# P times V in three fused layers: from two fp32r products with split operands to one float32 product, two heads on the two 64-column halves of TensorE

## The chip, the cores and the metric

One core of a Trainium2 chip runs the whole program. The metric is device time in microseconds (us), taken as the median of several runs. The engines are named as in the profile: PE is TensorE (its matmuls), PEld its weight loads, DVE is VectorE, ACT is ScalarE, POOL is GpSimd, and SP is SyncE, which here only issues DMAs.

## What is computed

Three layers follow one another: an attention whose keys are masked by a hash, a mixture of four causal attention experts (moe), and a mixing layer with sines (moe2). In short form:

```python
def _attn_ref(q, k, v, proj):            # q, k, v: (2, 8, 768, 64), proj: (64, 6)
    q_bits = (np.einsum('bhsd,dk->bhsk', q, proj) > 0)
    k_bits = (np.einsum('bhsd,dk->bhsk', k, proj) > 0)
    mask = q_bucket[:, :, :, None] == k_bucket[:, :, None, :]
    scores = np.where(mask, scale * np.matmul(q, k.transpose(0, 1, 3, 2)), -1e9)
    attn = np.exp(scores - scores.max(-1)); attn /= attn.sum(-1) + 1e-09
    return np.matmul(attn, v)
def _moe_ref(x, w_gate, wq, wk, wv, wo): # x: (2, 768, 512), four experts of width 64
    for e in range(4):                   # causal attention of each expert, two of four kept
        ye = softmax(causal(q @ k.T)) @ v @ wo[e]
        out += gate(x, e) * ye
def _moe2_ref(x, w_theta, w_tok_r, w_tok_i, w_ch):
    theta = x @ w_theta
    y = w_tok_r @ (x * cos(theta)) + w_tok_i @ (x * sin(theta))
    return (x + y) + np.maximum((x + y) @ w_ch, 0.0)
```

## The kernel before

**Two heads are a group.** The attention has 2 batches of 8 heads, so 8 groups; the moe has 2 batches of 4 experts, so 4 groups. A group has 6 row blocks of 128 queries for each head (or expert), called side 0 and side 1. A `Unit` is one such row block in the attention; in the moe it is one row block of each side, whose widths differ because of the causal mask.

**What a unit does.** `scores` (L2009) multiplies queries and keys in PSUM with operands in fp32r, each number split into a high and a low part that are packed into the 128 rows of one operand; 12 further rows hold the hash bits of q and k, so that the mask comes out of the same product. `low` (L2018, DVE) scales the scores and takes the row's extreme, `exp` (L2027, ACT) makes P. `flip` (L2035) transposes P block by block on PE into PSUM. `split_hi` (L2046, ACT) rounds the transposed P to fp32r as PTh, `split_lo` (L2049, DVE) writes the rest as PTl. `mix` (L2065, PE) multiplies: V is stationary with 128 columns, 64 of its high part and 64 of its low part, and PTh and PTl stream through it in turn, 256 columns (two row blocks) at a time. So the result O holds, for one head, two halves of 64 partitions that still have to be added. `gather` copies O out of PSUM (ACT), `swap` (L1959, a DMA on SP's queue) brings one half onto the other's partitions, and `add` (L1963, mostly POOL) adds them into `bt`. `scale`, `spread` and `finish` divide by the sums.

**Preparation.** For each pair of heads `Prep` loads q, k and v, splits q and k on POOL, computes the hash with 8 fp32r matmuls (L2220: high and low parts of q and k against split projection weights), turns it into bits on ACT (L2222), DVE (L2224) and POOL (L2225), splits V into its high and low halves on POOL (`values`, L2233 and L2234), and packs the operands with DMAs on SP's queue (L2243). The very first pair is handled apart (`first_head`); its hash is the one place where PE multiplies plain float32 (L2161 to L2186). In the moe, `values_b` splits V on ACT and DVE, and for batch 0 both are parked in DRAM (`v_d`).

**What sets the order.** The program text gives a default order of jobs (`fill`, `ORD`). A planner (`Plan`) then reads all instructions with prices for each kind (`price`), schedules them by list with a rank of how far each lies from the end, and fixes the order on every engine. A long table `NUDGES` shifts the ranks of instructions in certain stretches of time before the last pass of that planner. Pools of tiles limit what may be alive: three PSUM tiles `ps`, two tiles `O`, two pairs PTh and PTl. Idle places of PE at the very start are filled with 38 spare matmuls (L1902).

## Time and profile before

| | |
|---|---|
| time, median of 3 runs | 530.48 us (530.31 to 530.82) |
| span of the profiled execution | 527.9 us, so some 2.6 us of the median lie around it |
| PE busy (ends modelled) | 520.5 us, 99% |
| PEld (weight loads, beside PE) | 458.9 us, 87% |
| DVE / ACT / POOL busy | 427.0 / 370.7 / 294.6 us |
| L2065, P times V on PE | 768 matmuls |
| L2049 and L2046, the split of P transposed | 116.6 us of DVE, 97.9 us of ACT |
| L1963, the adding of the halves | 42.4 us of POOL |

Matmuls are pipelined: one of 256 columns has a record of about 0.3 us, but the next begins some 0.12 us later. So PE's busy share says little, and the distance from start to start says what a matmul costs. The view that shows it is the chain of work that ended last, where matmuls in a row are merged with their number. The stages are: attention up to about 260 us (with the projections of the first moe batch inside it), the moe up to about 355 us, then the mixing layer.

### The profile page before, as it was taken

Reading aid. Unit: us, or ns where it says so; the run is one execution under the profiler, and the core shown is the slowest. Engines: PE = TensorE matmul, PEld = TensorE weight load, DVE = VectorE, ACT = ScalarE, POOL = GpSimd, SP = SyncE. Lnnn points to the kernel's source line nnn. Section 1 sums busy time; section 2 is a strip of 40 time slices with the busy share of each in tenths; the row PEclk is TensorE's granted clock in tenths of the full one; section 3 lists DMA queues with packets and bytes.
Section 4 is the critical chain, followed back from the end, with each engine's and each line's share of the span. In section 5 each row is a group of like instructions: output and inputs, shape, how many; then the busy total and the mean of one; then the engine's idle time right before and its main releaser. Section 6 shows DMA issues by size and latency. Waiting matters only on the chain.

```text
span 527.9 us, 9485 instructions
## 1 busy us (share of the span) xinstructions
PE 520.5 (99%) x3341; PEld 458.9 (87%) x3341; DVE 427.0 (81%) x707; ACT 370.7 (70%) x691; POOL 294.6 (56%) x248
## 2 busy tenths in 40 slices
PE   9999999999999999999999999999999999999997
PEld 5999999979999999999898998878888778888886
DVE  6898988898987699888967988988989999924343
ACT  7888888888755588778968668996775667553110
POOL 6988998539504798824230204746766487955000
PEclk9999999999999999999999999999999999999999
DMA  6774644637477764795716533653445343350012
GB/s 205 194 191 143 170 131 108 181 73 194 135 257 241 236 190 128 181 243 135 196 54 188 144 122 97 178 156 91 112 117 170 120 120 120 88 153 20 20 61 99
DMA packets 33287, 76.04 MB, mean 144 GB/s; under 512 B 6000, under 2 KB 7664, under 8 KB 33240
## 3 DMA queue, kind: packets, MB, share of 16 engines
q1 hardware_dynamic: 31080, 71.94, 48.8%
q10 hardware_dynamic: 2160, 3.50, 1.8%
q8 instruction: 26, 0.43, 0.3%
q14 instruction: 21, 0.17, 0.1%
HBM read 44.67 MB, written 14.32 MB: 112 GB/s over the span
## 4 chain that ended last, share of the span: by engine, by line
PE 89%; DVE 3%; ACT 2%; issue 2%; DMA 2%; POOL 1%; POOLq 0%; ACTq 0%
PE ps L2638 18%; PE ps L2009 15%; PE O L2065 15%; PE ps L2035 14%; PE ps L2357 6%; PE wk L2552 5%; PE wk L2567 4%; PE ps L2292 3%; PE ps L2567 3%; PE ps L2220 2%; PE ps L2499 1%; DMA raw<-in_wtok_dram 1%; PE spare L1902 1%; DMA bt<-ob 1%; PE wk L2651 1%
## 5 line engine op out<-in xcount | busy, mean ns | idle before, releaser
L2018 DVE TENSOR_SCALAR_CACHE_REDUCE ss<-ps 128x768 f32<-128x768 f32 (+3 forms) x144 | 119.3, 840 | 26.2 <-PE ps L2009 16.2
L2027 ACT ACTIVATE ss<-ss,m 128x768 f32<-128x768 f32 (+4 forms) x144 | 122.3, 850 | 15.3 <-DVE ss L2018 14.7
L2049 DVE TENSOR_TENSOR PTl<-ps,PTh 128x768 fp32r<-128x768 f32 x120 | 116.6, 980 | 10.9 <-ACT PTh L2046 10.5
L2046 ACT CAST PTh<-ps 128x768 fp32r<-128x768 f32 x120 | 97.9, 819 | 29.6 <-PE ps L2035 23.5
L2035 PE MATMUL ps<-ident,ss 128*128 128x128 f32 x744 | 109.7, 273 | 0.8 <-DVE PTl L2049 0.6
L2065 PE MATMUL O<-PTh,V 128*128 128x256 f32 (+1 forms) x384 | 104.7, 296 | 0.0
L2065 PE MATMUL O<-PTl,V 128*128 128x256 f32 (+1 forms) x384 | 103.4, 293 | 0.0
L1963 POOL TENSOR_TENSOR bt<-bt,ob 64x768 f32<-64x768 f32 x23 | 42.4, 1845 | 86.8 <-DMA bt<-ob 37.3
L2035 PEld LDWEIGHTS ps<-ident,ss 128*128 128x128 f32 x744 | 85.8, 140 | 4.3 <-PE O L2065 0.6
L2638 PE MATMUL ps<-zh,tok 128*128 128x512 f32 x240 | 77.8, 394 | 0.0
L2065 PEld LDWEIGHTS O<-PTh,V 128*128 128x128 f32 x384 | 72.6, 189 | 2.1 <-ACT PTh L2046 0.2
L2065 PEld LDWEIGHTS O<-PTl,V 128*128 128x128 f32 x384 | 72.9, 190 | 1.5
L2009 PE MATMUL ps<-op 76*128 76x256 f32 (+5 forms) x256 | 63.8, 341 | 0.2 <-DVE PTl L2049 0.2
L2638 PEld LDWEIGHTS ps<-zh,tok 128*128 128x128 f32 x240 | 44.8, 188 | 9.3
L2638 PE MATMUL ps<-zl,tok 128*128 128x512 f32 x120 | 46.7, 396 | 0.5 <-DVE zl L2599 0.5
L1834 POOL TENSOR_TENSOR tok<-raw,tok 128x512 fp32r<-128x512 f32 x27 | 40.7, 1518 | 8.6 <-ACT tok L1831 6.5
L2009 PEld LDWEIGHTS ps<-op 128*128 128x128 f32 (+1 forms) x256 | 41.0, 190 | 3.5 <-DVE PTl L2049 0.4
L2638 PEld LDWEIGHTS ps<-zl,tok 128*128 128x128 f32 x120 | 22.5, 188 | 6.0 <-DVE zl L2599 1.3
L2027 ACT ACTIVATION_READ_ACCUMULATOR ss<-ss,m 128x1 f32 x144 | 27.5, 191 | 0.0
L1808 DVE SCALAR_TENSOR_TENSOR g<-raw,g 128x512 uint32<-128x512 uint32 x26 | 26.8, 1032 | 0.4
L2587 POOL TENSOR_TENSOR kk<-kk,x 128x512 f32<-128x512 f32 x12 | 17.3, 1443 | 17.4 <-ACT kk L2586 14.0
L1809 DVE SCALAR_TENSOR_TENSOR g<-raw,g 128x512 uint32<-128x512 uint32 x26 | 25.5, 981 | 0.5
(241 smaller groups left out, 1100.9 us busy)
## 6 DMA issues: line engine op xcount, KB each, us to landing
raw<-in_wtok_dram SPq DMA_DIRECT2D x18, 512.0 KB
raw<-tok_d SPq DMA_DIRECT2D x27, 256.0 KB
bt<-ob SPq DMA_DIRECT2D x24, 192.0 KB
tok_d<-g SPq DMA_DIRECT2D x18, 256.0 KB
op<-qk_d SPq DMA_DIRECT2D x24, 192.0 KB
rT<-r_d SPq DMA_DIRECT2D x20, 192.0 KB
raw<-in_vP_dram SPq DMA_DIRECT2D x8, 384.0 KB
qk_d<-op SPq DMA_DIRECT2D x8, 384.0 KB
```

Of the source, the lines that this page charges most:

```text
L1834: nc.gpsimd.tensor_sub(l, raw, f(h))
L1963: engine.tensor_add(self.bt[keep], self.bt[keep], self.ob[keep, side])
L2009: nc.tensor.matmul(self.sp[:, c0:c1], lhs, rhs[:, c0 - off:c1 - off], start=a == 0, stop=last)
L2018: i = nc.vector.tensor_scalar(self.ss[:, off:off + w], self.sp[:, off:off + w], -0.125, NEG, op0=OP.mult, op1=OP.min, accum_out=m)
L2027: e = nc.scalar.activation(self.P[:, off:off + w], self.ss[:, off:off + w], AF.Exp, bias=m, scale=-1.0, accum_out=self.grp.den[:, side, i: ...
L2035: nc.tensor.transpose(self.pt[:, j * 128:(j + 1) * 128], self.P[:, j * 128:(j + 1) * 128], ident)
L2046: nc.scalar.copy(self.d[0], self.v)
L2049: nc.vector.tensor_sub(self.d[1], self.v, f(self.d[0]))
L2065: nc.tensor.matmul(o, g.V[:, j, side, :], rhs, start=j == 0 and a == 0, stop=j == w // 128 - 1 and a == 1)
L2357: nc.tensor.matmul(pp[:, c0:c1], lhs[:, kd, e, :], rhs[kd][:, c0:c1], start=n == 0, stop=n == 3 * NK - 1)
L2567: nc.tensor.matmul(o, lhs[:, sl], rhs[:, kd, cols], start=n == 0, stop=n == 3 * NK - 1)
L2638: nc.tensor.matmul(yp[t], lhs[:, a, t, :], rhs[:, a], start=i == 0 and a == 0 and n == 0, stop=i == NT - 1 and a == 1 and n == 2)
```

## The change

**P times V.** Transposed P is copied once, as float32, from PSUM to a tile PT (`copy`): of three units two are copied by ACT and one by DVE. V is not split: the attention loads it straight into the tile that PE reads; the moe copies it out of PSUM in one instruction on ACT. `mix` multiplies in float32 with V of one head as stationary operand, 64 columns wide, and writes it to one half of O's partitions; side 0 to partitions 0 to 63, side 1 to 64 to 127. The matmuls of the two sides alternate. All matmuls of one such product (12 in the attention; 12, 8 and 4 in a moe group) are glued: the planner lets nothing of PE between them, and the first waits for all that any of them needs. A product now needs both heads, so the order of the row blocks changes (`LINE0`, `LINE1`, `LINE2`). No halves have to be added: `swap`, `add` and `bt` are gone.

**Hash.** For all pairs but the first, four float32 matmuls of 384 columns read raw q and k, each with 32 weight columns on its own 32 partitions of PSUM, and one DVE instruction makes the bits. Each row of bits is now in two pieces, so there are twice as many small DMAs into the operands.

**Planner.** Prices for float32 matmuls on 64 and 32 columns, the glue, and an empty `NUDGES`.

The diff, cut to its core:

```diff
-NUDGES = [
...
+NUDGES = []
...
         if o.dt.endswith("float32"):
-            return 4 * n * 0.45, 4 * n * 0.45 + 160
+            s = 4 * n / 2.4
+            return s * {32: 0.25, 64: 0.5}.get(parts, 1.08), s + 180
...
+        for run in runs:
+            ns = [number[i.name] for i in run]
...
+            ops[ns[0]].step += SWITCH
+            ops[ns[-1]].step += SWITCH
...
-        def swap(self, side):
-            keep, mov = halves(side)
-            nc.sync.dma_start(self.bt[keep], self.ob[mov, side])
-
-        def add(self, engine, side):
-            keep, _ = halves(side)
-            engine.tensor_add(self.bt[keep], self.bt[keep], self.ob[keep, side])
...
+        def copy(self):
...
+            if units.index(self) % COPIES:
+                nc.scalar.copy(rs.PT[:, rs.n:rs.n + nb, :], src)
             else:
...
-            nc.scalar.copy(self.d[0], self.v)
-
-        def split_lo(self):
-            nc.vector.tensor_sub(self.d[1], self.v, f(self.d[0]))
+                nc.vector.tensor_copy(rs.PT[:, rs.n:rs.n + nb, :], src)
...
-                for j in range(w // 128):
-                    for a in range(2):
-                        if j < w0 // 128:
-                            rhs, o = self.PT[a][:, a0 + j:a1 + j + 1:a1 - a0, :], O
-                        else:
-                            rhs, o = self.PT[a][:, a1 + j, :], O[:, 1, :]
-                        nc.tensor.matmul(o, g.V[:, j, side, :], rhs, start=j == 0 and a == 0,
-                                         stop=j == w // 128 - 1 and a == 1)
...
+            for j in range(n1):
+                for side in (0, 1):
+                    (PT, a0), (_, a1) = g.at[side, 2 * c], g.at[side, 2 * c + 1]
+                    half = slice(side * 64, side * 64 + 64)
+                    if j < n0:
+                        rhs, o = PT[:, a0 + j:a1 + j + 1:a1 - a0, :], self.O[half]
+                    else:
+                        rhs, o = PT[:, a1 + j, :], self.O[half, 1]
+                    together(nc.tensor.matmul(o, g.V[:, j, side, :], rhs, start=j == 0, stop=j == n1 - 1),
+                             j == side == 0)
...
         def hash(self):
-            qh, ql, kh, kl = self.s
             hp = ps_tile()
-            for a, (lhs, rhs) in enumerate(((hq, qh), (hq, ql), (hk, kh), (hk, kl))):
-                for c0, c1 in cuts(S):
-                    nc.tensor.matmul(hp[:, c0:c1], lhs, rhs[:, c0:c1], start=a == 0, stop=a == 3)
-            nlo = hold.tile([128, S], F32, name="nlo", tag="x", bufs=2)
-            nc.scalar.activation(nlo[0:64], hp[64:128, :S], AF.Copy, scale=-1.0)
-            bits = early.tile([64, S], F32R, name="bits", tag="bits", bufs=1)
-            nc.vector.tensor_tensor(out=bits, in0=hp[0:64, :S], in1=nlo[0:64], op=OP.is_gt)
-            nc.gpsimd.tensor_scalar(bits, f(bits), bc[:, 0:1], bc[:, 1:2], op0=OP.add, op1=OP.mult)
-            self.bits = bits
...
+            for n, raw in enumerate((self.qr, self.qr, self.kr, self.kr)):
+                c = n % 2 * 384
+                together(nc.tensor.matmul(hp[n * 32:n * 32 + 32, 0:384], hw[:, n // 2 * 32:n // 2 * 32 + 32],
+                                          raw[:, c:c + 384], start=True, stop=True), n == 0)
+            self.bits = early.tile([128, S], F32R, name="bits", tag="bits", bufs=1)[:, 0:384]
+            nc.vector.tensor_scalar(self.bits, hp[:, 0:384], hl[:, 0:1], hl[:, 1:2], op0=OP.is_gt, op1=OP.mult)
```

**Where instructions stand.** PE's queue in the first attention group, before: `O` is the result of P times V, `PTh` and `PTl` the two parts of transposed P, `ss` the P that is transposed, and the rows of L2009 are scores of later units.

```order
L2065 MATMUL O_313<-PTl_346,V_234 128x256
L2009 MATMUL ps_424<-skh_205,sql_202 128x512
L2009 MATMUL ps_424<-skh_205,sql_202 128x256
L2009 MATMUL ps_424<-op_270,op_269 128x512
L2009 MATMUL ps_424<-op_270,op_269 128x256
L2065 MATMUL O_313<-PTh_345,V_234 128x256
L2035 MATMUL ps_432<-ident_58,ss_356 128x128 x6
L2065 MATMUL O_313<-PTl_346,V_234 128x256
L2065 MATMUL O_313<-PTh_345,V_234 128x256
L2065 MATMUL O_313<-PTl_346,V_234 128x256
```

The same queue after, from the transposes whose copy the first product waits for (`ps_359` becomes part of `PT_369`) to its first matmuls; eight more of L975 follow in the same way.

```order
L946 MATMUL ps_359<-ident_58,ss_324 128x128 x6
L920 MATMUL ps_371<-op_168,op_167 128x512
L920 MATMUL ps_371<-op_168,op_167 128x256
L920 MATMUL ps_371<-op_170,op_169 128x512
L920 MATMUL ps_377<-op_168,op_167 128x512
L920 MATMUL ps_377<-op_168,op_167 128x256
L920 MATMUL ps_371<-op_170,op_169 128x256
L920 MATMUL ps_377<-op_170,op_169 128x512
L946 MATMUL ps_403<-ident_58,ss_348 128x128 x6
L920 MATMUL ps_377<-op_170,op_169 128x256
L975 MATMUL O_413<-PT_287,V_196 64x256
L975 MATMUL O_413<-PT_369,V_196 64x256
```

The P times V matmuls, which stood between scores and transposes one by one, now stand in an unbroken row, and 36 such rows and 7 rows of hash matmuls stand between full-width matmuls.

DVE's queue at the same place, before: L2018 works on scores, L2049 makes PTl, L2224 hash bits.

```order
L2018 TENSOR_SCALAR ss_439,m_440<-ps_424 128x768
L2049 TENSOR_TENSOR PTl_430<-ps_396,PTh_429 128x768
L2049 TENSOR_TENSOR PTl_430<-ps_432,PTh_429 128x768
L2018 TENSOR_SCALAR ss_458,m_459<-ps_444 128x768
L2049 TENSOR_TENSOR PTl_475<-ps_451,PTh_474 128x768
L2018 TENSOR_SCALAR ss_494,m_495<-ps_477 128x768
L2049 TENSOR_TENSOR PTl_475<-ps_485,PTh_474 128x768
L2018 TENSOR_SCALAR ss_512,m_513<-ps_498 128x768
```

And after, where L929 works on scores and L957 copies one of three transposed units.

```order
L957 COPY PT_334<-ps_327 128x768
L929 TENSOR_SCALAR ss_348,m_349<-ps_337 128x768
L929 TENSOR_SCALAR ss_366,m_367<-ps_343 128x768
L929 TENSOR_SCALAR ss_410,m_411<-ps_371 128x768
L957 COPY PT_426<-ps_403 128x768
L929 TENSOR_SCALAR ss_429,m_430<-ps_377 128x768
L929 TENSOR_SCALAR ss_455,m_456<-ps_442 128x768
L929 TENSOR_SCALAR ss_486,m_487<-ps_458 128x768
```

Every second instruction of DVE was one that finished a split; now every third or fourth is a copy, and a copy needs PE's transpose alone, not ACT's instruction before it.

PE's queue at a hash, before (`hq`, `hk` are the split projection weights, `sq..` and `sk..` the split q and k):

```order
L2220 MATMUL ps_757<-sqh_520,hq_98 128x512
L2220 MATMUL ps_757<-sqh_520,hq_98 128x256
L2220 MATMUL ps_757<-sql_521,hq_98 128x512
L2220 MATMUL ps_757<-sql_521,hq_98 128x256
L2220 MATMUL ps_757<-skh_524,hk_99 128x512
L2220 MATMUL ps_757<-skh_524,hk_99 128x256
L2220 MATMUL ps_757<-skl_525,hk_99 128x512
```

And after, with the scores ahead of it and the transposes and the product behind it:

```order
L920 MATMUL ps_628<-op_390,op_389 128x512
L920 MATMUL ps_628<-op_390,op_389 128x256
L1112 MATMUL ps_635<-raw_268,hw_98 32x384 x2
L1112 MATMUL ps_635<-raw_267,hw_98 32x384 x2
L946 MATMUL ps_667<-ident_58,ss_607 128x128 x6
L975 MATMUL O_674<-PT_589,V_321 64x256
```

Eight matmuls that needed POOL's four splits first are now four that need only the raw loads.

## Rows read from the trace of the kernel before

**Rows 1.** The page: busy time of each engine; chain's shares by engine.

```profile
PE 520.5 (99%) x3341; PEld 458.9 (87%) x3341; DVE 427.0 (81%) x707; ACT 370.7 (70%) x691; POOL 294.6 (56%) x248
...
PE 89%; DVE 3%; ACT 2%; issue 2%; DMA 2%; POOL 1%; POOLq 0%; ACTq 0%
```

**Rows 2.** Chain in order of time: start us, length us, engine, tile, line, count.

```profile
13.90 1.31 PE ps L2035 x12
...
25.02 0.83 PE O L2065 x7
...
74.51 1.41 PE ps L2220 x8
...
106.90 0.87 DVE PTl L2049
...
115.09 0.88 DVE PTl L2049
...
318.63 4.59 DMA bt<-ob
323.39 1.81 POOL bt L1963
...
346.61 0.91 ACT PTh L2046
...
362.02 3.73 PE ps L2638 x16
```

**Rows 3.** PE's groups by shape: count, busy us, mean ns of a record, idle before.

```profile
L2035 PE MATMUL ps<-ident,ss 128*128 128x128 f32 x744 | 109.7, 273 | 0.8 <-DVE PTl L2049 0.6
L2065 PE MATMUL O<-PTh,V 128*128 128x256 f32 x360 | 100.4, 300 | 0.0
L2065 PE MATMUL O<-PTl,V 128*128 128x256 f32 x360 | 98.5, 294 | 0.0
...
L2065 PE MATMUL O<-PTl,V 128*128 128x128 f32 x24 | 6.5, 271 | 0.0
...
L2567 PE MATMUL ps<-wcl,uTh 128*128 128x256 f32 x8 | 2.1, 281 | 0.0
```

**Rows 4.** Stretches: PE, PEld, DVE, ACT, POOL busy us (count), granted clock, DMA share, GB/s.

```profile
20.00:60.00 40.00, 40.00 (x305) 38.00 (x304) 35.20 (x60) 34.51 (x62) 35.28 (x37) 1.00 0.62 166
...
100.00:120.00 20.00, 19.40 (x134) 16.81 (x133) 18.43 (x30) 16.09 (x29) 9.41 (x9) 1.00 0.32 79
...
340.00:360.00 20.00, 18.76 (x125) 16.27 (x124) 16.55 (x30) 18.28 (x38) 9.32 (x8) 1.00 0.49 153
```

**Rows 5.** Timeline of PE, 3 to 14 us: start, length, line, form (rows*columns of weights), records.

```profile
6.29 0.59 PE L2170 MATMUL ps<-raw,start 128*76 128x256 f32 x2
6.72 0.59 PE L2171 MATMUL ps<-raw,start 128*76 128x256 f32 x2
7.15 0.38 PE L1902 MATMUL spare<-identb 128*128 128x256 bf16 x2
...
8.66 0.94 PE L2009 MATMUL ps<-op 76*128 76x512 f32 x4
9.44 1.02 PE L2186 MATMUL ps<-raw,start 128*76 128x512 f32 x2
10.30 1.15 PE L1902 MATMUL spare<-identb 128*128 128x256 bf16 x9
```

**Rows 6.** Timeline of weight loads, 3 to 12 us.

```profile
9.32 0.26 PEld L2186 LDWEIGHTS ps<-raw,start 128*76 128x76 f32 x2
```

**Rows 7.** Groups of the other engines: count, busy us, mean ns, idle before, its releaser.

```profile
L2049 DVE TENSOR_TENSOR PTl<-ps,PTh 128x768 fp32r<-128x768 f32 x120 | 116.6, 980 | 10.9 <-ACT PTh L2046 10.5
...
L2046 ACT CAST PTh<-ps 128x768 fp32r<-128x768 f32 x120 | 97.9, 819 | 29.6 <-PE ps L2035 23.5
...
L1963 POOL TENSOR_TENSOR bt<-bt,ob 64x768 f32<-64x768 f32 x23 | 42.4, 1845 | 86.8 <-DMA bt<-ob 37.3
...
L2224 DVE TENSOR_TENSOR bits<-ps,nlo 64x768 fp32r<-64x768 f32 x7 | 6.6, 947 | 0.1
```

More of the change, by code (lines that the diff above doesn't have):

```diff
@@ L47 @@
 LATE = [0, 2, 1, 2, 2, 2, 2, 5, 5, 5]
-ORD = 'SFYLHEKGMX'
+ORD = 'SFYLHEGMX'
 ONACT2=8
@@ L1424, with __init__ @@
 class Plan:
-    def __init__(self, nc, tc, waits, turns, free=()):
+    def __init__(self, nc, tc, waits, turns, runs=(), free=()):
         self.ops, self.users, info = read_program(nc, tc)
@@ L1435, in __init__ @@
             ops[number[late.name]].need.setdefault(number[early.name], "data")
+        self.glue = {}
+        for run in runs:
+            ns = [number[i.name] for i in run]
+            inside = set(ns)
+            for a, b in zip(ns, ns[1:]):
+                self.glue[a] = b
+                ops[b].need[a] = "order"
+            for n in ns[1:]:
+                for k, v in ops[n].need.items():
+                    if k not in inside:
+                        ops[ns[0]].need.setdefault(k, v)
+            ops[ns[0]].step += SWITCH
+            ops[ns[-1]].step += SWITCH
+            ops[ns[0]].late += SWITCH
         self.spare = [o.n for o in ops if o.tiles and o.tiles[-1].startswith("spare")]
@@ L1510, in forward @@
         lanes = []
+        bound = None
         for _ in self.todo:
@@ L1514, in forward @@
                 could = []
-                for n in heads[e]:
+                for n in heads[e] if e != "PE" or bound is None else [bound]:
                     at = max(free[e], ready[n])
@@ L1554, in forward @@
             order[e].append(n)
+            if e == "PE":
+                bound = self.glue.get(n)
             for name in self.limited[n]:
@@ L1758, in fused @@
 @with_exitstack
-def fused(ctx: ExitStack, tc: tile.TileContext, qT, kT, vP, projd, wqk_d, wvg, wo, woT, wth, wtok, wch, out, waits, turns, desk,
-          families, sequence):
+def fused(ctx: ExitStack, tc: tile.TileContext, qT, kT, vP, projd, wqk_d, wvg, wo, woT, wth, wtok, wch, out, waits, turns, runs,
+          desk, families, sequence):
     nc = tc.nc
@@ L1780, in in_turn, with together @@
         turns.append(ins.ins)
+    def together(ins, new):
+        if new:
+            runs.append([])
+        runs[-1].append(ins.ins)
     def hi_pool(dst, src):
@@ L1930, in __init__ @@
             self.ob = self.rp = None
-            self.pairs = 0
-            self.PT = {}
+            self.at, self.done, self.ended = {}, set(), set()
         def scale(self, gw=None, away=True):
@@ L1994, in __init__ @@
             self.w = off
+            grp.done |= {(side, i) for side, i in rows}
+            ends = [c for c in range(NT // 2) if c not in grp.ended
+                    and {(s, 2 * c + a) for s in (0, 1) for a in (0, 1)} <= grp.done]
+            self.ends = ends[0] if ends else None
+            grp.ended |= set(ends)
         def scores(self):
@@ L2067, in mix @@
-            self.O = g.O
-            self.pair = g.pairs
-            g.pairs += 1
+            c = self.ends
+            self.O = ps.tile([128, 2, 128], F32, name="O", tag="O", bufs=2)
+            n0, n1 = (2 * c + 1, 2 * c + 2) if g.causal else (NT, NT)
+            for j in range(n1):
[8 more added lines that the diff above has]
+                             j == side == 0)
@@ L2623, in fused @@
             one = {"S": far, "L": far, "E": far, "M": last, "G": prev}.get(what, near)
-            if one and (one.before or what not in "MG"):
-                jobs.append((getattr(one, {"S": "scores", "L": "low", "E": "exp", "F": "flip", "H": "split_hi",
-                                         "K": "split_lo", "M": "mix", "G": "gather"}[what]), ()))
+            if one and (one.ends is not None or what not in "MG"):
+                jobs.append((getattr(one, {"S": "scores", "L": "low", "E": "exp", "F": "flip", "H": "copy",
+                                         "M": "mix", "G": "gather"}[what]), ()))
     assert not fill
@@ L2779 @@
                     break
-                plan = Plan(nc, tc, waits, turns, FREE)
+                plan = Plan(nc, tc, waits, turns, runs, FREE)
                 t, order, reuse = plan.arrange(SLACK, 6, NUDGES)
```

198 lines of the change are left out of this document (85 added, 113 removed), and 1115 rows, old and new, of the table NUDGES.

## The prediction

> **What bounds the kernel now.** I read the busy times first, then the chain that ended last, then PE's groups, and last the stretches. PE is busy for 99% and the chain runs on PE for 89% of the span [rows 1]; no other engine comes near, DVE being next with 81% [rows 1]. So the question is how much of PE's queue the change takes away, and whether PE really is never kept waiting. The busy share cannot tell the second, since a record of about 0.30 us [rows 3] covers the next start. The chain can: seven matmuls of P times V take 0.83 us, so one costs 0.118 us [rows 2]. In the same way a transpose costs 1.31/12 = 0.109 us, a matmul of 512 columns 3.73/16 = 0.233 us, and the eight of a hash 1.41 us [rows 2]. If each of PE's groups, from the transposes to the smallest of 256 columns [rows 3], is multiplied by its step (0.233 for 512 columns, 0.175 for 384, 0.118 for 256 and 260, 0.109 for transposes, 0.07 as an estimate for 128), the sum is 511 us, an estimate. Of the span of 527.9 us PE thus loses about 17 us. Some 6.5 of these are start and end, which the change doesn't touch. By the same sum over stretches of 20 us, 100 to 120 us loses 2.6 us (134 matmuls there, against 305 in the 40 us from 20 on [rows 4]) and 320 to 360 us loses 5; the rest is spread. The granted clock is 1.00 in every stretch, the upper level of 2.4 GHz [rows 4], so nothing is to be won or lost there as long as PE keeps its queue full.
>
> I make the sum against 530.5 us: the span of 527.9 and the 2.6 around it, which is the median.
>
> **Term A, P times V on PE.** It removes 720 matmuls of 256 columns and 48 of 128 [rows 3]: 720 x 0.118 + 48 x 0.07 = 88.4 us. It adds 360 float32 matmuls of 256 columns and 24 of 128, each for 64 columns of weights. What a float32 matmul costs shows at the first hash: each is two records, and from the first of L2170 to the first of L2171 to the next matmul it is 0.43 us twice, so 0.215 us for each pass over 256 columns [rows 5]. One after another the new ones would take 360 x 0.43 + 24 x 0.215 = 160 us. Those at the first hash are 76 columns wide, so they use both halves of the array, and no row shows two matmuls side by side. The lower bound is that the two heads overlap wholly: 80 us. If the passes of the queue still begin strictly in turn, pass 1 of a row of matmuls runs alone, later ones in pairs, and each of the 36 rows costs about 0.2 us more: 87 us. The upper bound is 160. I take 80, and put what a row loses at its edges into term C. A = 80 - 88.4 = -8.4 us.
>
> Beside this stands the Trainium skill. Its page TensorEngine Tiling (Array Packing), Key Properties, says that tiles work independently and that loads and matmuls of different tiles run in parallel; by that, term A is the 80 us. Its page TensorE: Matmul & The Clock Gate, Part 3, gives 2.38 times for three column tiles; as an estimate from that page two halves would then give about 1.6 times, and 160/1.6 = 100 us, so A = +12. No row here shows either.
>
> **Term B, the hash.** Seven times 1.41 us are removed [rows 2], 9.9 us. Four matmuls of 384 columns take 0.43 x 1.5 = 0.645 us each by [rows 5]: all four side by side 0.645 x 7 = 4.5 us, one after another 18.1 us. If passes begin in turn, two at a time overlap and a hash takes five passes of 0.32 us, 11.3 us for all. I take 8, between the first and the last of these. B = -1.9 us.
>
> **Term C, the edges.** 36 rows of products and 7 of hash matmuls stand between full-width matmuls, which makes 86 changes of shape. The nearest row is a change from fp32r to float32 without any change of width: the four matmuls of L2009 that start at 8.66 cost 0.70 us by their steps, so L2186 could start at 9.36 and starts at 9.44 [rows 5], with its weights loaded from 9.32 on [rows 6]: 0.08 us. From float32 to the next it is nothing: L2186 ends its two passes of 0.43 us at 10.30, where the next starts [rows 5]. The upper bound is a full emptying of the pipe, 0.30 - 0.118 = 0.18 us of a record [rows 3], and one exposed load on top, 0.26 in all. The lower bound is nothing. I take 0.08, the only change of form that is shown: C = 86 x 0.08 = +6.9 us; the ends are 0 and +22.4.
>
> **Term D, PE's waits.** What vanishes from the chain are the split of transposed P (DVE at 106.90 and 115.09 us, ACT at 346.61), the DMA of the halves with 4.59 us and the adding of them with 1.81 us at 318.63 [rows 2]. DVE loses 116.6 us of PTl and gets 42 copies; a copy out of PSUM of the same size took ACT 0.82 us and the subtraction 0.98 [rows 7], so about 38 us come back. ACT goes from 120 such copies to 82. POOL loses 42.4 us of adding [rows 7], the V splits and the bits. All that was not on PE and in itself is worth nothing. It counts where DVE held PE up, from 100 to 120 us, where it was 18.43 of 20 us busy [rows 4], and in part of 320 to 360. Of the 10.5 us that PE loses between start and end I let 6 go: D = -6 us. What is late next at 326.59 are 3.03 us of the chain's "issue" [rows 2] and the weights of the mixing layer behind it, which the change leaves, so not all goes. The bounds are -10.5 (all) and +6 (below).
>
> **Nothing on the path.** A row of products is glued: its first matmul waits for the copies of both heads, and behind it in PE's queue stand the next unit's transposes. At the first product eight score matmuls (four pairs of 512 and 256, 1.4 us) and six transposes (0.65 us) lie between the last transposes it needs and itself, and the copy takes 0.82 us on ACT; the cover is 1.2 us wide, less if ACT first has another copy or an exp. If it is gone, PE waits up to 0.9 us at each of 36 rows. V unsplit comes with the load and is ready earlier. On SP's queue 24 DMAs of halves go and 28 small ones of bits come; the bits themselves are ready earlier, since one DVE instruction of half the columns (0.95 us for 768 [rows 7]) stands for three on three engines.
>
> **The sum.** 530.5 - 8.4 - 1.9 + 6.9 - 6.0 = 521.1 us.
>
> **Rivals.**
> 1. *The edges cost more than the halves give.* Each change of shape empties the pipe (0.18 us, 15.5 us for 86) and each row's first pass runs alone (A = 87 - 88.4 = -1.4, B = 11.3 - 9.9 = +1.4): 530.5 - 1.4 + 1.4 + 15.5 - 6 = 540 us, and 547 with a load exposed at each (22.4). For it: a record lasts 0.18 us beyond its step [rows 3], and nothing in PE's queue hides it if the array has to be empty. Against: the one change of form shown cost 0.08. It makes the kernel slower from about 0.15 us for each change on. The Trainium skill speaks for it: its page TensorEngine Tiling (Array Packing), Key Properties, says that a change of tiling mode drains TensorE. No row shows such a change.
> 2. *The order is worse.* The table of rank shifts is empty and a glued row waits for the last of four copies; PE's waits then grow by 6 instead of shrinking by 6: 530.5 - 8.4 - 1.9 + 6.9 + 6 = 533 us, or about no change if they only stay. For it: the waits now are small, so the order before fits its work closely. Against: every other engine has less to do.
> 3. *The halves overlap, their weight loads don't.* If a half loads its next weights only after its own pass, a pair costs two times 0.215 + 0.13 (two loads took 0.26 [rows 6]), 0.69 us: 180 x 0.69 + 12 x 0.48 = 130 us, A = +41.6, time 530.5 + 41.6 - 1.9 + 6.9 - 6 = 571 us. Against: at the first hash a second load lies wholly beside the first pass [rows 5, 6].
> 4. *The halves don't overlap*, so the change doesn't do what it says: A = 160 - 88.4 = +71.6, B = 18.1 - 9.9 = +8.2, C and D as above: 611 us. For it: no row shows an overlap.
>
> **The numbers.** The forecast has 0.62, its own range is 505 (A and B at their low ends, no edge cost, all waits gone: 530.5 - 8.4 - 5.4 - 10.5 = 506) to 529. Rival 1 has 0.15, rival 2 0.12 (of which 0.07 within 0.2%), rival 3 0.04, rival 4 0.07. 0.2%, or about 1 us, is what a measurement of this kernel can tell from no change. So faster has 0.62, the same 0.07, slower 0.15 + 0.05 + 0.04 + 0.07 = 0.31. The range reaches from 505 to 548, the upper end of rival 1; it leaves out rivals 3 and 4 and a little on either side.
>
> **What would show it.** In the trace of the changed kernel: a row of 12 products should take about 6 x 0.43 = 2.6 us from its first start to the next full-width matmul; 2.8 to 3.2 means rival 1, 3.6 and more rival 3, 5.2 rival 4. A hash should take 0.65 to 1.6 us. The chain should have no DVE piece near 110 us. Waits of PE for copies of PT would mean rival 2. The forecast is wrong if a row of products takes more than about 3 us or if PE's share of the chain falls below 85%.

## The result, and the profile after

The changed kernel takes 533.88 us (532.90 to 535.21, five runs); the kernel before took 530.82 us beside it. The ratio, with its 95% interval in brackets as everywhere below, is 1.0058 [1.0041, 1.0075]: slower by 0.6%, where 521 us and "faster" were forecast. The profiled execution of the changed kernel is the slowest of the five (535.21 us, span 533.4); its granted clock is 0.997 of the upper level over the whole span, that of the other four 0.999 to 1.000.

The page of the changed kernel: busy time of each engine, and the shares of the chain that ended last (they answer to [rows 1]).

```profile
PE 521.8 (98%) x3341; PEld 412.0 (77%) x3341; DVE 348.8 (65%) x613; ACT 330.4 (62%) x636; POOL 223.2 (42%) x186
...
PE 85%; DVE 8%; issue 2%; ACT 2%; DMA 1%; POOL 0%; DVEq 0%; SPq 0%; ACTq 0%
```

The other engines became as light as intended: DVE lost 78 us, ACT 40, POOL 71. Yet the chain now spends 8% on DVE instead of 3%, and PE's share fell from 89 to 85%. PE has become more dependent on an engine that has less to do. Most of the new share is one place: some 26 us of DVE's pieces in the chain lie between 400 and 435 us, in the mixing layer, whose work the change leaves; before, that place has 3 us.

The chain of the changed kernel in order of time, its pieces of the new products and the new hash with work right behind such rows and elsewhere, and pieces that are not on PE (start us, length us, engine, tile, line, count; they answer to [rows 2]):

```profile
28.43 2.74 PE O L975 x24
...
50.31 0.78 PE ps L1112 x8
...
111.33 0.84 ACT ss L938
...
114.22 0.97 DVE ss L929 x2
...
262.22 2.74 PE O L975 x24
264.96 0.70 PE ps L946 x5
...
266.78 0.55 PE ps L946 x5
...
271.79 2.53 PE O L975 x24
...
277.43 3.89 PE ps L1239 x22
...
282.99 1.66 PE O L975 x16
284.65 4.44 PE ps L1239 x24
...
429.65 1.71 DVE rr L1455
...
432.72 1.76 DVE zl L1476
```

A row of 12 products (24 records) takes 2.74 us in the attention, 2.53 in the moe, a moe row of 8 1.66 us, and a hash 0.78 us, where it took 1.41. What stands right behind a row is slower too: five transposes take 0.70 us there and 0.55 elsewhere, and 24 matmuls of L1239 take 4.44 us where 22 elsewhere take 3.89 (4.24 for 24). So a row costs 0.15 to 0.20 us behind it as well; behind a hash it is about 0.15 (six transposes in 0.80 us at 105.18 us, 0.66 elsewhere).

Its groups by line (form, count, busy us, mean ns of one, idle time before and what ended it; they answer to [rows 3] and [rows 7]):

```profile
L975 PE MATMUL O<-PT,V 128*64 128x256 f32 (+1 forms) x768 | 88.3, 377 | 0.0
...
L955 ACT COPY PT<-ps 128x768 f32<-128x768 f32 (+2 forms) x82 | 64.8, 796 | 30.8 <-PE ps L946 30.5
...
L957 DVE COPY PT<-ps 128x768 f32<-128x768 f32 (+2 forms) x42 | 39.9, 949 | 5.9 <-PE ps L946 5.9
```

The copies of PT wait for PE's transposes (30.5 and 5.9 us), not the other way round. DVE's largest group, the extremes of the scores, in the changed kernel and then in the kernel before:

```profile
L929 DVE TENSOR_SCALAR_CACHE_REDUCE ss<-ps 128x768 f32<-128x768 f32 (+3 forms) x144 | 119.5, 842 | 77.8 <-PE ps L920 44.8
```

```profile
L2018 DVE TENSOR_SCALAR_CACHE_REDUCE ss<-ps 128x768 f32<-128x768 f32 (+3 forms) x144 | 119.3, 840 | 26.2 <-PE ps L2009 16.2
```

DVE is idle for 77.8 us instead of 26.2 ahead of this step, mostly because PE hasn't made the scores: it gets its work later than it could take it, which by itself costs PE nothing.

What PE waited for (line, releaser, us in total, times, longest):

```profile
PE ps L920 <- DVE ss L929: 2.5, 7, 0.5
PE ps L1515 <- DVE zl L1476: 1.8, 1, 1.8
...
PE ps L920 <- DMA op<-bits: 1.0, 1, 1.0
PE ps L920 <- DVE op L1257: 0.7, 1, 0.7
```

And by stretches (PE, PEld, DVE, ACT, POOL busy us with counts, granted clock, DMA share, GB/s; they answer to [rows 4]):

```profile
20.00:60.00 40.00, 38.77 (x285) 29.21 (x285) 23.75 (x47) 26.83 (x51) 11.08 (x11) 1.00 0.42 106
...
100.00:120.00 20.00, 19.58 (x146) 14.49 (x145) 15.00 (x28) 14.72 (x28) 9.71 (x8) 1.00 0.41 127
```

From 100 to 120 us DVE went from 18.43 to 15.00 us and PE runs 146 matmuls instead of 134: the narrow place of before is wider. It isn't gone: the chain still leaves PE there, for ACT at 111.33 and for DVE at 114.22 us, where by the prediction's signs it should have no DVE piece. And from 20 to 60 us, where PE was busy without a gap [rows 4], it is now busy for 38.77 of 40 us although DVE is busy for 24 us instead of 35. Between 420 and 440 us, where PE waits for `zl`, the granted clock of this execution falls to a mean of 0.91 of the upper level (2.4 GHz); up to 520 us every other stretch of 20 us has 1.00.

**The account.** With the prediction's own steps (511 us of steps before), the products take 24 x 2.74 + 4 x (2.53 + 1.66 + 0.80) = 85.7 us instead of 88.4 and the hash 7 x 0.78 = 5.5 instead of 9.9; that leaves 503.9 us. The 0.80 us are the moe's rows of 4. Before, the span lost 527.9 - 511 = 17 us beside the steps; after it loses 533.4 - 503.9 = 29.5, and about 28 in the median execution, by its time. So PE has 7 us less to do and loses 11 us more. Some 7 of the 11 are lost in the work right behind the 43 rows (36 x 0.15 to 0.20 and 7 x 0.15), about 4 in waits. The pages agree: PE is idle for 527.9 - 520.5 = 7.4 us before and for 533.4 - 521.8 = 11.6 after.

### The profile page after: what moved, and what is told of

Same layout as the page of the kernel before. It is cut to its first block, busy times and chain, and to the rows that moved or that the text cites. A ratio compares the mean times of both kernels' runs of the same rounds, so it can differ in the third digit from the quotient of the medians.

```text
span 533.4 us, 9160 instructions
## 1 busy us (share of the span) xinstructions
PE 521.8 (98%) x3341; PEld 412.0 (77%) x3341; DVE 348.8 (65%) x613; ACT 330.4 (62%) x636; POOL 223.2 (42%) x186
## 4 chain that ended last, share of the span: by engine, by line
PE 85%; DVE 8%; issue 2%; ACT 2%; DMA 1%; POOL 0%; DVEq 0%; SPq 0%; ACTq 0%
PE ps L920 16%; PE O L975 16%; PE ps L1515 15%; PE ps L946 14%; PE ps L1239 6%; PE wk L1444 4%; PE wk L1429 3%; PE ps L1178 3%; PE ps L1444 3%; DVE ss L929 2%; DVE zl L1476 1%; PE ps L1376 1%; DVE g L721 1%; PE ps L1112 1%; PE ps L1429 1%
## 5 line engine op out<-in xcount | busy, mean ns | idle before, releaser
L929 DVE TENSOR_SCALAR_CACHE_REDUCE ss<-ps 128x768 f32<-128x768 f32 (+3 forms) x144 | 119.5, 842 | 77.8 <-PE ps L920 44.8
L938 ACT ACTIVATE ss<-ss,m 128x768 f32<-128x768 f32 (+3 forms) x144 | 121.6, 846 | 37.1 <-DVE ss L929 36.3
L975 PE MATMUL O<-PT,V 128*64 128x256 f32 (+1 forms) x768 | 88.3, 377 | 0.0
L955 ACT COPY PT<-ps 128x768 f32<-128x768 f32 (+2 forms) x82 | 64.8, 796 | 30.8 <-PE ps L946 30.5
L975 PEld LDWEIGHTS O<-PT,V 128*64 128x64 f32 x768 | 51.9, 137 | 29.5 <-issue 6.3
L920 PE MATMUL ps<-op 128*128 128x512 f32 (+5 forms) x256 | 61.4, 345 | 2.5 <-DMA op<-bits 1.0
L957 DVE COPY PT<-ps 128x768 f32<-128x768 f32 (+2 forms) x42 | 39.9, 949 | 5.9 <-PE ps L946 5.9
L983 ACT COPY ob<-O 128x256 f32<-128x256 f32 x36 | 13.3, 370 | 20.2 <-PE O L975 20.1
L920 PE MATMUL ps<-skh,op 128*128 128x512 f32 x84 | 24.6, 373 | 1.0 <-DVE ss L929 1.0
L920 PE MATMUL ps<-op,sql 128*128 128x512 f32 x84 | 24.5, 372 | 1.0 <-DVE ss L929 0.9
L720 DVE TENSOR_SCALAR g<-g 128x512 uint32<-128x512 uint32 x26 | 17.1, 658 | 10.6 <-ACT g L719 10.5
```

The lines of the kernel that those rows point to most:

```text
L920: nc.tensor.matmul(self.sp[:, c0:c1], lhs, rhs[:, c0 - off:c1 - off], start=a == 0, stop=last)
L929: i = nc.vector.tensor_scalar(self.ss[:, off:off + w], self.sp[:, off:off + w], -0.125, NEG, op0=OP.mult, op1=OP.min, accum_out=m)
L938: e = nc.scalar.activation(self.P[:, off:off + w], self.ss[:, off:off + w], AF.Exp, bias=m, scale=-1.0, accum_out=self.grp.den[:, side, i: ...
L955: nc.scalar.copy(rs.PT[:, rs.n:rs.n + nb, :], src)
L957: nc.vector.tensor_copy(rs.PT[:, rs.n:rs.n + nb, :], src)
L975: together(nc.tensor.matmul(o, g.V[:, j, side, :], rhs, start=j == 0, stop=j == n1 - 1), j == side == 0)
```

## The experiments

Two theories. **Theory E:** the edges of the rows eat the gain. **Theory O:** the order does, that is, the lost table and rows that can't be broken make PE wait. Names that begin with b_ are the kernel before with an edit, those with a_ the changed kernel with an edit.

**1. The table alone.** In `before`, `NUDGES = []`.

> The kernel before, with the table of rank shifts emptied and nothing else. Theory O (the order: the changed kernel gave up a fitted order, and its waits of PE grew from about 20 to about 32 us): the table was worth 4 us or more, so this runs 535 to 540 us, with the same matmuls and more waits of PE. Theory E (the edges alone: 43 rows of narrow matmuls at about 0.25 us each, 10 us, ate the gain and the order is as good as before): the table is worth nothing, 530 to 531.5 us.

534.44 us, 1.0068 [1.0051, 1.0084]: the table is worth about 4 us in the kernel before (4.3 between the medians, 3.6 by the ratio). Without tables the two kernels stand at 534.4 and 533.9. So the change by itself brings nothing that can be told from noise, and the kernel is slower by about what the table was worth.

**2. The halves, one after the other.**

```diff
-            for j in range(n1):
-                for side in (0, 1):
+            for side in (0, 1):
+                for j in range(n1):
```

> The changed kernel, with the matmuls of a product in another order: all of head 0, then all of head 1, instead of in turn. If the overlap of the halves hangs on the turn (passes start in the order of the queue): a row of 12 takes 24 x 0.215 = 5.2 us instead of 2.74, in all about 75 us more, 605 to 612 us. If the two halves run side by side whatever the order: 534 us.

586.42 us (one run), between the two. A row takes 4.52 us:

```profile
28.14 4.52 PE O L975 x24
```

Stretches of 0.22 us along one row, of this line alone (length, busy us, number of records that lie in it, clock, DMA share, GB/s); a record lasts 0.384 us, so two or three in a stretch mean one start, four or five mean two:

```profile
28.30:28.51 0.22, 0.22 (x2) 1.00 1.11 242
...
29.59:29.81 0.22, 0.22 (x2) 1.00 0.99 199
...
30.24:30.46 0.22, 0.22 (x5) 1.00 0.00 0
...
31.54:31.75 0.22, 0.22 (x3) 1.00 0.00 0
```

The same along a row of the changed kernel:

```profile
28.79:29.01 0.22, 0.22 (x5) 1.00 1.03 213
```

So there the two heads start as pairs, one pair each 0.216 us, throughout: the overlap is whole. With the sides apart eight passes run alone, then four pairs, then eight alone: 20 x 0.216 us and the edges.

**3. No glue.** `together` does nothing, so the planner may put other work between the products.

> The changed kernel without the glue: the planner may put scores and transposes between the matmuls of a product, and no edge has a price. The queue then has 120 rows of narrow matmuls instead of 43, 54 of them of one matmul. Theory E (edges dear, about 0.25 us for each row, and a matmul without a partner costs 0.43 us alone): 77 x 0.25 = 19 us for edges and 54 x 0.215 = 12 us for missing partners, less some 5 us of waits, so about 555 to 565 us. Theory O in its strong form (the unbroken rows starve the other engines and cost more than their edges): 525 to 532 us.

563.45 us (one run). PE is 99% busy and waits for hardly anything, and it is 30 us slower: rows that are split up cost PE's own time, as theory E says. How much of it is edges and how much products without a partner (19 and 12 us were expected), this run doesn't tell.

**4. More rows, fewer rows.** a_half_glue glues each product in two halves (66 rows with the hashes, not 43) and prices a change at nothing (`SWITCH = 0`). a_long_rows glues two chunks of the attention (24 products) and the moe's last two (12), which makes 31 rows. a_moe_joined joins only the moe's, 39 rows.

```diff
-                             j == side == 0)
+                             side == 0 and j in (0, n1 // 2))
```

> The changed kernel with each product in two glued halves and no price on edges: 66 rows of narrow matmuls instead of 43, all with partners. The edges read from the trace of the changed kernel are about 0.3 us for each row (0.09 to enter, 0.05 at the first pair, 0.1 to leave, and up to 0.1 at the next full-width matmul). Theory E: 23 x 0.3 = 7 us more than the changed kernel, 540 to 542 us. With the two times 0.08 us of the prediction: 3.7 us more, 537.5 us. If shorter rows help the other engines by more than that: 534 us or less.

> The changed kernel with fewer, longer rows of products: in each attention group the rows of query chunks 0 and 1 are one glued row of 24 products, in each mixture group those of chunks 1 and 0 one of 12, so 24 rows instead of 36 and 31 changes into narrow tiles instead of 43. There are six buffers of transposed P instead of four. Theory E (the edges of a row are what eats the gain): a row's edges are 0.24 to 0.30 us in the trace, 12 fewer rows give 2.9 to 3.6 us, so 530.3 to 531 us beside 533.9. Theory O (the waits between rows and the other engines decide): a row of 24 lasts 5.4 us, in which VectorE and ScalarE get nothing new out of PSUM, and what the edges give is lost again in waits: 533 to 537 us. The splitting of rows in two (23 more rows, 0.11 us net each) would say 1.3 us less by the net price: 532.6.

> The changed kernel with only the mixture groups' last two rows joined (query chunks 1 and 0, 8 and 4 products, to one of 12): 4 rows fewer, none longer than 12 products, and a delay of one unit for the first part. Theory E: 4 x 0.24 to 0.35 us less: 532.5 to 532.9 beside 533.9. If joining rows costs by itself (the delay and the burst of copies), as the joined rows of 24 did (3.9 us for 12 fewer rows): 535 us.

a_half_glue takes 536.39 us (1.0116 [1.0098, 1.0134]), a_long_rows 537.75 us (1.0144 [1.0127, 1.0161]) and a_moe_joined 534.87 us (1.0091 [1.0073, 1.0110]), which isn't clear of the changed kernel. More rows cost 2.5 us, where 7 were expected of their edges: by the pages PE is busy for 526.4 us instead of 521.8 and idle for 8.1 instead of 11.6. So the edges do cost PE's time, and shorter rows give part of it back in waits. But fewer rows cost too (a_long_rows at a granted clock of 0.996 to 0.997). A long row of 24 products in the chain of a_long_rows is

```profile
32.50 5.33 PE O L979 x48
```

that is 0.15 us less than two of 2.74, and from 120 to 260 us PE then runs 961 matmuls instead of 1007. The chain of a_long_rows is on PE for 62% and on DVE for 18%, where the changed kernel has 85% and 8%. So theory E alone is wrong: an unbroken row starves the engines behind PE, and theirs is the work that PE waits for next.

**5. The row without the halves.** The kernel before without its table, each pair's fp32r products glued; no tile is narrow.

```diff
-                        nc.tensor.matmul(o, g.V[:, j, side, :], rhs, start=j == 0 and a == 0,
-                                         stop=j == w // 128 - 1 and a == 1)
+                        together(nc.tensor.matmul(o, g.V[:, j, side, :], rhs, start=j == 0 and a == 0,
+                                                  stop=j == w // 128 - 1 and a == 1), a == j == 0)
```

> The kernel before without its table of shifts, with the fp32r products of P times V of each pair of units glued into one unbroken row (66 rows, 52 of them of 12 products or 1.4 us). No tile is narrow, so no edge is paid. Without glue this kernel took 534.4 us, with its products spread over 163 rows. Theory O: the spreading of the products is filler that hides the waits of other work, and glue costs 2 to 4 us: 536 to 538 us. Theory E: only the change into narrow tiles costs something, and glue by itself nothing: 534 to 535 us.

564.22 us, 30 us more than without glue, far beyond what either theory gave. What PE waits for in it:

```profile
PE ps L912 <- DVE ss L921: 7.9, 16, 1.8
PE ps L1260 <- DVE PTl L952: 3.1, 2, 2.9
PE ps L938 <- DVE ss L921: 2.8, 4, 1.4
```

Products spread singly were the filler that hid DVE's lateness. Edges are not the reason: five transposes behind such a full-width row take 0.55 us (at 245.29 us of its chain), as elsewhere. The same glue is bearable in the changed kernel, probably because DVE has lost its splits there; no run glues the old products beside a light DVE.

**6. The hash, each way round.** a_old_hash is the changed kernel with the hash of before. b_new_hash is the kernel before without table with the new hash; b_hash_kept has it too, but with the ranks that the table gives kept for every instruction that both have.

```diff
-            for a, (lhs, rhs) in enumerate(((hq, qh), (hq, ql), (hk, kh), (hk, kl))):
-                for c0, c1 in cuts(S):
-                    nc.tensor.matmul(hp[:, c0:c1], lhs, rhs[:, c0:c1], start=a == 0, stop=a == 3)
+            for n, raw in enumerate((self.qr, self.qr, self.kr, self.kr)):
+                c = n % 2 * 384
+                together(nc.tensor.matmul(hp[n * 32:n * 32 + 32, 0:384], hw[:, n // 2 * 32:n // 2 * 32 + 32],
+                                          raw[:, c:c + 384], start=True, stop=True), n == 0)
```

> The changed kernel with the hash of before: fp32r products of the split q and k over all 128 columns, the comparison on VectorE with a copy on ScalarE and a step on GpSimd; P times V stays as the change has it. In the traces a hash takes 1.41 us on TensorE before and 0.79 after, edges included, so if TensorE's queue sets the end, the seven hashes cost 7 x 0.62 = 4.3 us: 538.2 us beside 533.9. The rival is that the hash stands where TensorE has waits anyway or that the new one causes waits of its own (its row holds up what is behind it): no difference, 533 to 535 us.

> The same new hash in the kernel before, without the table of shifts. Without the table the kernel before took 534.4 us; with the hash's 3.7 to 4.3 us it should take 530 to 531 us. If it takes 534 us the new hash is worth something only beside the new P times V; if it is as fast as the same edit with the ranks of before kept, the table is worth nothing in this kernel.

> The kernel before with the new hash alone (raw q and k as float32 on four 32-column tiles); P times V stays as two fp32r products with the split. Every instruction that both have keeps the rank that the table of shifts gives it in the kernel before, so the order of before is kept in nearly all places (93% of TensorE's common instructions stand in the same order). By term B the seven hashes give 7 x (1.41 - 0.79) = 4.3 us, and undoing them alone cost the changed kernel 3.7 us: 526.5 to 527 us beside 530.5, if the order of before is worth its 4.3 us here too. The rival is that an order so fitted is lost by any edit, even with the ranks kept: 530 to 532 us, the same as without a table.

| without tables | old hash | new hash |
|---|---|---|
| old P times V | 534.4 | 537.6 |
| new P times V | 537.6 | 533.9 |

a_old_hash 537.59 us (1.0140 [1.0122, 1.0159]), b_new_hash 537.64 (1.0134 [1.0111, 1.0156]), b_hash_kept 533.59 (1.0065 [1.0047, 1.0084]). Beside the new products the hash gives 3.7 us, near what its steps promise (4.4, or 3.4 with the 0.15 us lost behind each). Beside the old ones it loses 3.6 with the table (533.6 against 530.0) and 3.2 without. The table's 4 us are there in both.

The clock has a part in the 3.2. Over the whole span the four executions of b_new_hash were granted 0.990 to 0.994 of the upper level and took 536.80 to 538.13 us; of b_no_table's five, three had 1.000 (533.11 to 534.44 us), and the one with 0.994 took 537.45. At a like clock, then, as far as that one execution tells, the hash gives nothing there rather than losing. In the profiled executions the two have made the same 590 transposes of P at 260 us. Then b_no_table's clock falls, to 0.95 to 0.97 up to 360 us, where b_new_hash is 27 matmuls ahead; at 440 us they are level again. In between PE waits for DVE in b_new_hash, and its clock falls to a mean of 0.96:

```profile
PE wk L1456 <- DVE rr L1481: 2.7, 1, 2.7
...
PE ps L1542 <- DVE x L1547: 1.7, 1, 1.7
```

```profile
360.00:440.00 80.00, 75.09 (x314) 60.36 (x313) 71.66 (x76) 52.10 (x92) 54.26 (x35) 0.96 0.44 130
```

The chain of b_hash_kept, whose clock is 0.999 to 1.000, shows another place where the hash's time isn't won:

```profile
110.05 0.81 ACT PTh L1261
110.86 0.03 issue
110.89 0.96 DVE PTl L1264
...
113.24 0.96 DVE ss L1233 x2
...
121.24 0.89 DVE ss L1233 x2
...
151.32 2.50 DMA op<-bits
```

From 110.89 to 122.13 us the chain is on DVE. Before, that piece ran from 105.94 to 115.97, and the old hash at 99 to 101 us was PE's work in front of it. PE now gets there earlier (at 105 us it has done 257 transposes instead of 252) and waits, since DVE has made 41 PTl by then in both kernels. At 151.32 us the chain goes over one of the 28 small DMAs of bits, which the prediction had put at nothing.

**7. DVE made light.** b_light is b_no_table without the subtraction that makes PTl; b_light_hash the same of b_new_hash. Both products read PTh.

```diff
-            nc.vector.tensor_sub(self.d[1], self.v, f(self.d[0]))
+            pass
```

> The kernel before without its table and without the subtraction that makes PTl on VectorE (both products of a pair read PTh, so P times V is not what the reference wants); TensorE's work is the same. VectorE loses 117 us of work. Term D of the prediction: if waits of TensorE for VectorE are what it loses between start and end, this alone gives about 4 to 6 us beside the 534.4 us of the same kernel with the subtraction: 528 to 530 us. The rival, that VectorE's load holds TensorE up nowhere once the order is free: 533 to 535 us.

> The same light kernel with the new hash. With the full load on VectorE the new hash made the kernel before 3.2 us slower (537.6 beside 534.4), beside the new P times V it made it 3.7 us faster. Theory O: TensorE's time saved by the hash counts where VectorE is not the bound, so here it should be 3 to 4 us faster than the light kernel with the old hash: 525 to 527 us. The rival, that the new hash's own waits (the small transfers of its bits, the held q and k) cost what it saves: as slow as the light kernel, or up to 3 us slower.

532.24 us (1.0057 [1.0035, 1.0079]) and 529.80 us (0.9994 [0.9985, 1.0003]). The hash's sign turns, from +3.2 to -2.4 us. At a like clock of 0.993 to 0.994 it goes from about nothing to -3.4 (531.92 to 532.24 us for b_light, 528.66 and 528.74 for b_light_hash), which is the 3 to 4 expected. DVE's load itself is worth only 2.2 us between the medians, and the stretches of b_light say why (columns as above):

```profile
100.00:120.00 20.00, 20.00 (x154) 19.04 (x153) 12.37 (x25) 17.29 (x33) 13.24 (x10) 1.00 0.40 101
...
360.00:440.00 80.00, 73.49 (x299) 58.48 (x298) 76.26 (x75) 48.05 (x84) 56.67 (x36) 0.94 0.44 130
```

Up to 360 us PE waits for almost nothing any more. Then it comes to the mixing layer before that layer's operands are made, runs 299 matmuls from 360 to 440 us where before ran 345, and its granted clock falls to a mean of 0.94 of the upper level. Beside the one execution of b_no_table that also had 0.994, b_light is 5 us faster. PE's waits in b_light_hash are of the same kind:

```profile
PE ps L1542 <- DVE z1l L1503: 3.5, 1, 3.5
PE ps L1542 <- POOL tok L738: 1.9, 1, 1.9
```

**8. Another order for the changed kernel.** a_table gives it, and b_new_table the kernel before, a table of shifts found with the planner's prices. a_head0_first takes all row blocks of head 0 first in the first group (`LINE0`). a_joined_head0 adds the joined moe rows, a_joined_copies lets ACT make three of four copies of PT (`COPIES = 4`), a_tuned2 besides moves places of the preparation, the projections and the mixing layer in the program text:

```diff
-LP = [2, 4, 5.5, 3, 7, 7, 9, 13, 9, 15, 16, 16]
+LP = [2, 4, 5.5, 3, 7, 6, 9, 13, 9, 15.5, 16, 16]
-PREP1 = [15, 10.5, 3.0, 4, 8]
-FIN = [-2, -2, 3.5, 5]
-MFIN = [0, 3, 3.5, 4, 4]
+PREP1 = [16, 10.5, 3.0, 3, 8]
+FIN = [-2, 0, 3.5, 5]
+MFIN = [0, 3, 2.5, 4, 4]
...
-M0F = [-6, -5, 4, -4, 0, 2]
+M0F = [-7, -5, 4, -4, -2, 2]
...
-ORD = 'SFYLHEGMX'
+ORD = 'SLYFHEGMX'
```

> The changed kernel with a table of rank shifts of its own, searched for with the planner's prices; 43 rows of narrow matmuls as in the changed kernel. Theory O (the missing table costs the changed kernel as much as it costs the kernel before, which ran 534.4 us without and 530.1 with it): 3.5 to 6 us less than the changed kernel, 528 to 530.5 us. Theory E (only the edges of the rows matter, some 0.3 us for each of 43): the edges stay, so 533 to 534.5 us.

> The kernel before with its table replaced by one found with the same search and as much of it as in a_table, so that both kernels stand on the same footing. Theory O: 528 to 531 us, about as with its own table; then the change itself is worth 0 to 1 us. If the change itself saves several us of PE's queue, as its 7 us shorter sum of steps says, this stays 3 us or more above a_table.

> The changed kernel, with the row blocks of the first group in another order: all six of head 0 first, then head 1, so that the packed operands of head 1 are needed after six units and not after four. Theory O: the first 60 us, where PE loses some 6 us in the changed kernel, lose 2 to 3 us less: 531 to 532 us. Theory E: no change, 533.5 to 534.5 us. If the products, which need both heads, are then held up instead, slower: 535 us or more.

> The same with the first group's units in the order of all of head 0 first, which by itself gave 532.9 us: 531.5 to 532 us by theory E; the two edits would add up. 533 to 536 us if the order's chance decides more than either.

> The changed kernel with all of head 0 first and the mixture groups' last rows joined (531.5 us), and now three of four copies of transposed P on ScalarE instead of two of three. VectorE then has a tenth fewer of its instructions ahead of the extremes of the scores, for which TensorE waits 2.5 us in seven places. If these waits go, 529 to 530 us; if ScalarE, which then has 90 copies beside its exponentials, becomes late in their place, 532 to 533 us.

> The same with the places of the preparation, the mixture's projections and the mixing layer in the program text moved by up to two units, found with the planner's own prices. By the kernels timed so far, a lower end in the planner's prices went with a lower time (519.5, 521.0, 523.8, 525.2 and 529.3 by the planner stood beside 532.9, 531.5, 533.9, 534.9 and 537.8 us on the chip); this one's is 511.6. If that holds, 524 to 527 us, faster than the kernel before. If an order found by these prices alone is worth nothing on the chip, as the two tables so found were, 531 to 534 us.

| | us | ratio to before |
|---|---|---|
| a_table | 534.25 | 1.0073 [1.0055, 1.0090] |
| b_new_table | 535.64 | 1.0100 [1.0084, 1.0116] |
| a_head0_first | 532.92 | 1.0049 [1.0033, 1.0064] |
| a_joined_head0 | 531.46 | 1.0026 [1.0012, 1.0041] |
| a_joined_copies | 528.89 | 0.9973 [0.9962, 0.9985] |
| a_tuned2 | 523.41 | 0.9884 [0.9864, 0.9904] |

The tables gave nothing in either kernel, so the 4.3 us of the table before were not made again. The three small moves gave 5.0 us together (the first alone, 1.0 us, isn't clear of noise) and the places another 5.5. a_tuned2 does the arithmetic of the changed kernel and beats both. Its page (engines, chain) and its waits:

```profile
PE 514.8 (99%) x3341; PEld 410.5 (79%) x3341; DVE 342.6 (66%) x602; ACT 336.5 (65%) x647; POOL 222.0 (43%) x186
...
PE 92%; DVE 3%; ACT 3%; DMA 1%; issue 0%; SPq 0%; DVEq 0%; ACTq 0%
```

```profile
PE ps L806 <- DVE warm L810: 1.2, 1, 1.2
PE ps L923 <- DVE ss L932: 0.9, 2, 0.5
PE wk L1433 <- ACT ob L987: 0.9, 1, 0.9
PE ps L949 <- DVE bits L1119: 0.4, 1, 0.4
```

The waits for DVE's `ss` fell from 2.5 to 0.9 us and that for the mixing layer's `zl` (1.8) is gone; the chain is on PE for 92%, and PE is idle for 6.9 us. With about the same 503.9 us of steps the span of 521.7 us loses 18 us, about as much as the kernel before, though some 7 of these are now lost behind rows.

## Why the prediction was wrong

Two steps failed: the price of an edge (term C), which was half of what it is, and the sign of PE's waits (term D).

- **Term A held.** The halves overlap wholly: a pair each 0.216 us, 180 x 2 x 0.216 and the short ones make about 80.4 us, so -8.0 against -8.4. The 100 us that were estimated from the Trainium skill's page TensorE: Matmul & The Clock Gate, Part 3, are refuted. The rule of the Trainium skill's page TensorEngine Tiling (Array Packing), Key Properties, that tiles work independently, agrees with the trace. Rivals 3 and 4 are out.
- **Term B was too small.** A hash takes 0.78 us and about 0.15 behind it, 0.93 in all, so -3.4 us where -1.9 was taken. Undoing it cost 3.7 us. That the hash would bring nothing beside the old products, where DVE is the bound, the prediction didn't see.
- **Term C failed in size.** A row should take 12 x 0.216 = 2.59 us and takes 2.74; what follows it loses another 0.15 (transposes) to 0.20 (other matmuls). That is 0.30 to 0.35 us a row, or 0.15 to 0.18 for each change, where 0.08 was taken, "the only change of form that is shown"; but that was a change without a change of width. For the 36 rows, 19 of them followed by transposes, it is about +11.7 us instead of 36 x 2 x 0.08 = 5.8, an estimate from these lines (the hash's edges are in its 0.93). So each change costs what rival 1 named as its limit, 0.15 us, or a little more; its other half, a first pass that runs alone, didn't come. The Trainium skill's page TensorEngine Tiling (Array Packing), Key Properties, says that a change of tiling mode drains TensorE; the trace agrees in that each change costs these 0.15 to 0.18 us. A and C together are about +3.7: the new products cost PE more than the old ones, and A, B and C together are about nothing (+0.3).
- **Term D failed, in sign.** -6 was taken; with A, B and C at about nothing the measured +3.1 leaves about +3, which fits PE's idle time (7.4 to 11.6 us, in an execution 1.3 us slower than the median). This is rival 2's mechanism, half as large, and that the time came within 1 us of its 533 is chance: rival 2 has the edges at 6.9 and the waits at +6. Its sign didn't show either: PE hardly waits for PT's copies, but for DVE's `ss`, the bits and the mixing layer. Another sign did speak against the forecast: the chain still has DVE pieces near 110 us. The rest were weak: a row of 2.74 us lies between the forecast's 2.6 and rival 1's 2.8, and PE's share of the chain is at the 85% below which the forecast was to be wrong. The step that failed is "every other engine has less to do" as an argument against rival 2. The argument has something in it, since a light DVE can take PE's waits away: b_light shows that up to 360 us, and a_tuned2 ends at 523.4 us, 6.8 below the kernel before, which with its 32 rows (A, B and C at about -1) is a D of about -6, as forecast. But the waits don't go of themselves. The order was fitted to the old loads (about 4 us of it in the table), and the new one has rows of 2.74 us in which nothing else may run. How the +3 divides between the two isn't shown.
- **"Nothing on the path"** was right for the copies, wrong for the small DMAs of bits (1.0 us of PE's waits; 2.50 us of the chain in b_hash_kept).

What stays open: why shifting places in the text gave 5.5 us where shifting ranks gave nothing, which of these places matter, and whether the kernel before would gain from the same search of places, which wasn't tried. So 523.4 us shows what the change can reach, not what it is worth against an equally searched kernel before.

## What to carry to other kernels

Work taken from the engine that bounds the kernel counts only where no second engine stands close behind it; read the stretch, and ask whose work the removed instructions were hiding. Price an edit that changes the order of a fitted kernel with the fit it loses (here about 4 us, more than the edit gave), and fit again before judging it. Price a change of width at what both sides of it lose; a change of data type alone is no measure for it (0.08 us here against 0.15 to 0.18). A new shape of matmul is best glued, but a row must stay short enough that the engines it feeds don't run dry: here 12 products were better than 6 or 24.

## What was not expected of the hardware

- With the sides apart, a row of 24 passes took 4.52 us, not the 5.2 of one after the other. The row begins at 28.14 us, so the twelve passes of the first side would be through at 28.14 + 12 x 0.216 = 30.73; the lines of experiment 2 show two starts in a stretch at 30.24 already, when passes of the first side that stand ahead in the queue have not begun. So across halves PE doesn't start matmuls strictly in turn. The Trainium skill's page TensorE: Matmul & The Clock Gate, Part 3, says that they start and end in program order; the trace differs.
- Four float32 matmuls on four 32-column tiles take 0.78 us with edges, where one of their size takes 0.645 by the first hash [rows 5]: all four run side by side.
